# Moving the factor gb and a row term off VectorE in the last phase of an adaLN forward-and-backward kernel

## The chip, the cores and the metric

The kernel runs on one core of a Trainium2 chip. The time is device microseconds of that core, as the median of the runs; the profile is one execution, whose span runs from its first to its last instruction. The engines are called as the profile calls them: PE (TensorE matmuls), PEld (its weight loads), DVE (VectorE), ACT (ScalarE), POOL (GpSimd) and SP (SyncE, which here only issues transfers).

## The reference, cut to what matters

One block is computed with its whole backward pass: a spectral filter and a two-layer MLP (squared relu), each behind a LayerNorm that is modulated by vectors from `silu(c) @ w_mod`.

```python
sa, ca, ga, sb, cb, gb = chunks(silu(c) @ w_mod)      # six rows of 512
h = layernorm(x) * (1 + ca) + sa
x = x + ga * spectral(h, w_r, w_i)                    # x: 2048 x 512
h = layernorm(x) * (1 + cb) + sb
r = relu(h @ w1 + b1)                                 # 2048 x 1792
x = x + gb * ((r * r) @ w2 + b2)
# outputs: x, and the gradients of A_x, w_r, w_i, w1, b1, w2, b2, c, w_mod for a given grad_out
```

Two gradients matter here. With g = grad_out (2048 x 512) and H = r*r:

- grad w2 = H^T (g * gb) and grad b2 = the column sums of g * gb. Since gb belongs to the column, it can be applied to g before the product, or to the product after it.
- grad A_x, the last phase, is the backward pass of the first LayerNorm. For each row, with n the normalized row, s its incoming gradient times (1 + ca) and times 1/std: grad = s - mean(s) - n * mean(s * n), plus the gradient that comes past the block. `n * factor + offset`, with a factor and an offset for each row, is the term of the change's name.

## The kernel before

The kernel keeps rows as 128 partitions x 16 tiles x 512. A scheduler orders each engine's instructions by priority and estimated readiness, so that the order on an engine is near that of the program but not the same; `issue_after(X)` keeps an instruction from being placed ahead of X. Tiles come from pools with a number of buffers (`bufs`). A pool that opens where another was released waits for the last user of that memory.

The stage before the last is the backward of the spectral filter (`spec_f23`, eight steps gi). PE fills its gaps with units of grad w1 (`fill_w1`, L1126), and the gradient of w_mod is made by `gm.emit`, for four of six column blocks here:

```python
def ew_b(gi, G):
    ...                                              # DVE complex products; gW is stored by SP
def after_b(gi):
    if gi + 4 < 8:
        load(gi + 4)
    if gi == 3:
        with tc.issue_after(K["gW"]):
            nc.sync.dma_start(K["LG"], LG_dram)
    fill_w1(2 if 0 < gi < 6 else 1)
    if gi == 4:
        with tc.issue_after(K["gW"]):
            load_hn()                                # a transposed load of H, 128 x 2048
            load_hn()
    if gi == 5:
        gmp.release()
        endp["g"] = tc.alloc_tile_pool(name="gsp", bufs=1, side="right")
        endp["g_sb"] = endp["g"].tile([P, NT, D], BF16, name="g_sb")
        with tc.issue_after(K["gW"]):
            K["g_load"] = nc.sync.dma_start(endp["g_sb"], g_view).ins
    if gi in (0, 1, 3, 4):
        gms.pop(0)[1]()                              # gm.emit of one block
        if len(gms) > 1:
            gm.load(gms[1][0], gmp)
```

Then come the units of grad w2, here with the factor gb on the product, and the loads of the last phase's rows:

```python
def grad_w2(fc):
    ps = mmps.tile([P, SB], FP32, name="mm")
    for t in range(NT):                              # L1203
        nc.tensor.matmul(ps, lhsT=hns[fc][:, t, :], rhs=g_sb[:, t, :], start=(t == 0), stop=(t == NT - 1))
    gw = gwp.tile([P, D], BF16, name="gw", bufs=3)
    with tc.high_priority():                         # L1206
        nc.vector.tensor_tensor(gw, ps, modb[:, GB_B, :], op=ALU.mult)
    nc.sync.dma_start(out6_view[:, fc, :], gw)
    load_hn()
...
with tc.issue_after(K["g_load"]):
    load_rows3(0)                                    # n1 and gxl, two row tiles each
    load_rows3(2)
for _ in range(2):
    load_hn()
CS = utcs.tile([P, NT, 4, 16, 8], BF16, name="utcs")
spec_g1(tc, K, Z, CS)                                # PE L346; casts of the result: DVE L351, ACT L353
```

The last phase is a loop over eight pairs of row tiles. `fill(n)` gives PE n units in between: three of grad w1 that are left, then the 14 of grad w2.

```python
def row_pair(t, Ts):
    n1, gxl = rows3[t]
    ...
    for i in range(2):
        psY = spec_g3(tc, K, Ts[i], psE)             # PE L385; Ts was cast by ACT, L377
        nc.scalar.copy(out=gs[:, i, :], in_=psY)     # ACT L1276
    unfold(nc, fp, gh1, gs, 2, "unf_u")              # DVE L266 to L270
    nc.vector.tensor_tensor(gn, gh1, modb[:, CA1_B, ...], op=ALU.mult)                   # L1278
    for i in range(2):                               # ACT L1280, with the row's sum
        nc.scalar.activation(gs[:, i, :], gn[:, i, :], AF.Copy, scale=inv1[...], accum_out=rr[:, i, 0:1])
    nc.vector.tensor_tensor(q1, gh1, n1, op=ALU.mult)                                    # L1281
    late.add(lambda: colsums1(t, gh1, q1))           # PE L1262
    for i in range(2):                               # L1285, the row's sum of s * n
        nc.vector.scalar_tensor_tensor(out=jk, in0=gs[:, i, :], ..., in1=n1[:, i, :], ..., accum_out=rr[:, i, 1:2])
    nc.vector.tensor_scalar(rr[:, :, 2:4], rr[:, :, 0:2], -1.0 / D, None, op0=ALU.mult)
    for i in range(2):                               # L1289
        nc.vector.tensor_scalar(gn[:, i, :], n1[:, i, :], rr[:, i, 3:4], rr[:, i, 2:3], op0=ALU.mult, op1=ALU.add)
    nc.vector.tensor_tensor(gs, gn, gs, op=ALU.add)                                      # L1290
    nc.vector.tensor_tensor(gx, gs, gxl, op=ALU.add)                                     # L1292
    nc.sync.dma_start(out1_view[:, t:t + 2, :], gx)
    load_rows3(t + 4)

Ts = g2_pair(0)                                      # PE L375, ACT L377
for t in range(0, NT, 2):
    fill(1)
    row_pair(t, Ts)
    Ts = g2_pair(t + 2)
    fill(1 if t % 4 == 0 and t < 12 else 0)
    if t == 10:
        grad_b2()
fill(1)
late.flush()
...                                                  # column sums acc1 -> acc1_sb
fill(1)
for j in range(2):                                   # the last two blocks of grad w_mod
    gm.load(j, endp["gm"])
    gm.emit(j, 32 * j, acc1_sb[32 * j:32 * j + 1, :], endp["gm"], psX)
    fill(1)
while units2:
    fill(1)
...                                                  # grad c
```

Of the kernel before, what the change touches and what calls it, by code (L numbers as in the profile page):

```python
# [9 lines left out]
AF = mybir.ActivationFunctionType  # L10
ALU = mybir.AluOpType
# [7 lines left out]
D = 512  # L19
# [313 lines left out]
        f3(7)  # L333


def spec_g1(tc, K, Z, CS):
    nc = tc.nc
    with tc.tile_pool(name="psG", bufs=4, space=PSUM) as psG_pool, tc.tile_pool(name="psF", bufs=1, space=PSUM) as psF_pool:
        psF = psF_pool.tile([P, 4, P], FP32, name="psF")
        for gi in range(8):  # L340
            for hh in range(2):
                n = 2 * gi + hh
                ps = psG_pool.tile([P, 2, 2 * P], FP32, name="psG")
                for ch in range(2):
                    for ri in range(2):
                        nc.tensor.matmul(ps[:, ch, :], lhsT=Z[gi][:, hh, ri, ch:256:2],  # L346
                                         rhs=K["LG"][:, n, ri:ri + 2, :].rearrange("p y m -> p (y m)"), start=(ri == 0), stop=(ri == 1))
                dst = CS[:, :, :, n, :].rearrange("p t c b -> p c t b")
                src = ps.rearrange("p h (y t b) -> p (h y) t b", y=2, b=8)
                if hh == 0:  # L350
                    nc.vector.tensor_copy(out=dst, in_=src)  # L351
                else:
                    nc.scalar.copy(out=dst, in_=src)  # L353

            if gi % 2 == 1:
                for ri in range(2):
                    for n in range(2 * gi - 2, 2 * gi + 2):
                        q = 32 * (n % 4)
                        nc.tensor.matmul(psF[q:q + 1, n // 4, :], lhsT=Z[n // 2][:, n % 2, ri, 256:257], rhs=K["LG"][:, n, ri + 1, :],
                                         start=(ri == 0), stop=(ri == 1), tile_position=(0, q))  # L360
        for i in range(4):
            dst = CS[0:1, :, 1, i:16:4, :].rearrange("p t m b -> p m t b")
            src = psF[32 * i:32 * i + 1, :, :].rearrange("p m (t b) -> p m t b", b=8)
            if i % 2 == 0:
                nc.vector.tensor_copy(out=dst, in_=src)
            else:
                nc.scalar.copy(out=dst, in_=src)
# [76 lines left out]
class GMod:  # L444
# [10 lines left out]
        for dc in range(0, 4, 2):  # L455
            self.tc.nc.sync.dma_start(self.tiles[jc][dc // 2], self.wm_view[:, dc:dc + 2, cs])

    def emit(self, jc, q, row, pool, ppool):

        nc, K = self.tc.nc, self.K  # L460
        cs = slice(jc * D, (jc + 1) * D)
        psb = ppool.tile([P, D], FP32, name="mm")
        nc.tensor.matmul(psb, lhsT=K["ones_sq"][q:q + 1, :], rhs=row, start=True, stop=True, tile_position=(q, 0))
        gmbc = pool.tile([P, D], BF16, name="gmbc", bufs=1)
        nc.scalar.copy(out=gmbc, in_=psb)  # L465
        junk = pool.tile([P, D], BF16, name="gm_junk", bufs=1)
        for dc in range(0, 4, 2):
            wmc = self.tiles[jc][dc // 2]
            gwm = pool.tile([P, 2, D], BF16, name="gwm", bufs=2)
            for i in range(2):  # L470
                if i == 0:
                    nc.scalar.activation(gwm[:, i, :], gmbc, AF.Copy, scale=self.scf[:, dc + i:dc + i + 1])
                else:
                    nc.vector.tensor_scalar(gwm[:, i, :], gmbc, self.scf[:, dc + i:dc + i + 1], None, op0=ALU.mult)
                nc.vector.scalar_tensor_tensor(out=junk, in0=wmc[:, i, :], scalar=K["onef"], in1=gmbc, op0=ALU.mult, op1=ALU.mult,  # L475
                                               accum_out=self.gsc[:, jc, dc + i:dc + i + 1])
            nc.gpsimd.dma_start(self.out9_view[:, dc:dc + 2, cs], gwm)  # L477
# [3 lines left out]
def kernel(  # L481
# [585 lines left out]
            nc.sync.dma_start(hns[fc], h_dram[fc, :, :], transpose=True)  # L1067

    lf2 = tc.alloc_tile_pool(name="lf2", bufs=1, side="right")
    gmp = tc.alloc_tile_pool(name="gmp", bufs=1, side="right")  # L1070
    K["LF"] += [lf2.tile([P, 2, 3, P], BF16, name=f"LFb{gi}") for gi in range(4, 8)]
    W4 = 448
# [17 lines left out]
        nc.scalar.copy(out=b4, in_=ps[:, 0:W4])  # L1090
        nc.gpsimd.dma_start(out_5.rearrange("(q f) -> q f", q=NFB), b4[0:P:32, :])

    def add_quadrants(ps, pool, out, scale=None):
        w = ps.shape[-1]
        b4 = pool.tile([P, w], BF16, name="b4", bufs=1)
        b4l = pool.tile([P, w], BF16, name="b4l", bufs=1)
        nc.scalar.copy(out=b4, in_=ps)
        nc.vector.tensor_tensor(b4l, ps, b4, op=ALU.subtract)

        def add():  # L1100
            ps = mmps.tile([P, SB], FP32, name="mm")
            for i, x in enumerate((b4, b4l)):
                nc.tensor.matmul(ps[0:1, 0:w], lhsT=K["ones_col"], rhs=x, start=(i == 0), stop=(i == 1))
            row = pool.tile([1, w], BF16, name="b4r", bufs=2)
            nc.scalar.copy(out=row, in_=ps[0:1, 0:w])
            if scale is not None:
                nc.vector.tensor_tensor(row, row, scale, op=ALU.mult)
            nc.sync.dma_start(out, row)

        later.append([4, add])  # L1110
# [3 lines left out]
    def run_later(n=1):  # L1114
        if later:
            later[0][0] -= n
            if later[0][0] <= 0:
                later.pop(0)[1]()

    w1o = {}  # L1120

# [27 lines left out]
    with tc.tile_pool(name="f23b", bufs=2) as fr, tc.tile_pool(name="ewb", bufs=2) as ew:  # L1149
# [22 lines left out]
# [3 lines that stand above are left out]
            if gi == 3:  # L1175
                with tc.issue_after(K["gW"]):
                    nc.sync.dma_start(K["LG"], LG_dram)
            fill_w1(2 if 0 < gi < 6 else 1)
            if gi == 4:
                with tc.issue_after(K["gW"]):  # L1180
                    load_hn()
                    load_hn()
            if gi == 5:
                gmp.release()
                endp["g"] = tc.alloc_tile_pool(name="gsp", bufs=1, side="right")
                endp["g_sb"] = endp["g"].tile([P, NT, D], BF16, name="g_sb")
                with tc.issue_after(K["gW"]):
                    K["g_load"] = nc.sync.dma_start(endp["g_sb"], g_view).ins
            if gi in (0, 1, 3, 4):
                gms.pop(0)[1]()  # L1190
                if len(gms) > 1:
                    gm.load(gms[1][0], gmp)

        spec_f23(tc, K, UT, AEs, None, lambda gi: gwa.tile([P, 2, 2, FP], BF16, name="G", bufs=2), ew_b, after_b)
    g_sb = endp["g_sb"]
    fin = tc.alloc_tile_pool(name="fin", bufs=2, side="right")
    gwp = tc.alloc_tile_pool(name="gwp", bufs=1, side="right")
    endp["gw"] = gwp

# [3 lines that stand above are left out]
            nc.tensor.matmul(ps, lhsT=hns[fc][:, t, :], rhs=g_sb[:, t, :], start=(t == 0), stop=(t == NT - 1))  # L1203
        gw = gwp.tile([P, D], BF16, name="gw", bufs=3)
        with tc.high_priority():
            nc.vector.tensor_tensor(gw, ps, modb[:, GB_B, :], op=ALU.mult)  # L1206
        nc.sync.dma_start(out6_view[:, fc, :], gw)
        load_hn()

    def grad_b2():  # L1210
        ps = psX.tile([P, D], FP32, name="mm")
        for t in range(NT):
            q = 32 * (t % 4)
            nc.tensor.matmul(ps[q:q + 32, :], lhsT=K["ones_q"], rhs=g_sb[:, t, :], start=(t < 4), stop=(t >= 12), tile_position=(0, q))
        add_quadrants(ps, gwp, out_7[None, :], modb[0:1, GB_B, :])

    rows3 = {}

    def load_rows3(t):
        if t < NT:  # L1220
            rows3[t] = (fin.tile([P, 2, D], BF16, name="n1"), fin.tile([P, 2, D], BF16, name="gxl"))
            nc.sync.dma_start(rows3[t][0], n1_dram[:, t:t + 2, :])
            nc.sync.dma_start(rows3[t][1], gx1_dram[:, t:t + 2, :])

    with tc.issue_after(K["g_load"]):
        load_rows3(0)
        load_rows3(2)
    for _ in range(2):
        load_hn()

    CS = utcs.tile([P, NT, 4, 16, 8], BF16, name="utcs")
    spec_g1(tc, K, Z, CS)
    sp.release()
    lg2.release()
    fp = tc.alloc_tile_pool(name="fin2", bufs=2, side="right")
# [19 lines left out]
    with tc.tile_pool(name="psE", bufs=2, space=PSUM) as psE, tc.tile_pool(name="psS1", bufs=1, space=PSUM) as psS1:  # L1255
# [11 lines left out]
        def row_pair(t, Ts):  # L1267
# [18 lines left out]
                                               accum_out=rr[:, i, 1:2])  # L1286
            nc.vector.tensor_scalar(rr[:, :, 2:4], rr[:, :, 0:2], -1.0 / D, None, op0=ALU.mult)
            for i in range(2):
                nc.vector.tensor_scalar(gn[:, i, :], n1[:, i, :], rr[:, i, 3:4], rr[:, i, 2:3], op0=ALU.mult, op1=ALU.add)  # L1289
            nc.vector.tensor_tensor(gs, gn, gs, op=ALU.add)  # L1290
            gx = fp.tile([P, 2, D], BF16, name="gx")
            nc.vector.tensor_tensor(gx, gs, gxl, op=ALU.add)  # L1292
# [4 lines left out]
        for t in range(0, NT, 2):  # L1297
# [3 lines left out]
            fill(1 if t % 4 == 0 and t < 12 else 0)  # L1301
            if t == 10:
                grad_b2()
        fill(1)
        late.flush()
        acc1_odd = fp.tile([64, D], FP32, name="acc1_odd", bufs=1)
# [2 lines left out]
        nc.vector.tensor_tensor(acc1_sb, acc1[0:64, :], acc1_odd, op=ALU.add)  # L1309
        fill(1)  # L1310
        for j in range(2):
            gm.load(j, endp["gm"])
            gm.emit(j, 32 * j, acc1_sb[32 * j:32 * j + 1, :], endp["gm"], psX)
            fill(1)
        while units2:
            fill(1)
# [10 lines left out]
    psX.release()  # L1327
    fp.release()
    gwp.release()
    fin.release()  # L1330
    endp["g"].release()
    lf2.release()
    hnp.release()
    h2p.release()
# [37 lines left out]
```

## Time and profile before

| | value |
|---|---|
| time, median of 3 | 429.94 us (428.81 to 430.19) |
| span of the profiled run | 428.8 us |
| busy PE, DVE, ACT | 396.5, 354.7, 256.5 us |
| bytes moved by transfers | 101.11 MB |
| span from L1126's last units to the end | 345.39 to 428.8 us |

The page gives busy shares over the whole span, and they hide that the stages differ. PE is busy 92% overall, DVE 83%; which of them sets the pace is to be read stage by stage. In a line of groups the columns are the line of the program, the engine, the operation, output and inputs by name, the shapes and the count; then the busy time in us and the mean of one in ns; then the idle time of the engine just ahead of them, with what ended it. In a timeline the first column is the start and the second the length, both in us, and idle time ahead of the piece stands in brackets. An engine works through its queue in order, so a piece that waits holds up all behind it.

### The profile page before, as it was taken

To read this page: it belongs to the slowest core of one execution; us is meant where nothing else is said; L and a number is where in the kernel's file an instruction comes from. 1 tells how busy PE (TensorE), PEld (TensorE's weight loads), DVE (VectorE), ACT (ScalarE), POOL (GpSimd) and SP (SyncE) were. 2 spreads that over 40 slices of the span, in tenths; PEclk is the share of its full clock that TensorE was granted. 3 is DMA by queue.
4 is the path that set the end of the run, shared out by engine and by line. 5 is a ranking of instruction groups with operands and counts; after the bars stand their busy time and mean duration, and the time that the engine had idled before them with its cause. 6 is when DMAs were issued, how large, how long until landed. Compare 5 with 4: busy or idle time off the path is not lost.

```text
span 428.8 us, 7116 instructions
## 1 busy us (share of the span) xinstructions
PE 396.5 (92%) x2353; PEld 195.9 (46%) x2375; DVE 354.7 (83%) x862; ACT 256.5 (60%) x487; POOL 54.7 (13%) x135
## 2 busy tenths in 40 slices
PE   2789999999899999999999999999999999998894
PEld 0345446654434444444444444455555654443341
DVE  6799858959995588978897998947997946999994
ACT  5568699778882188248734856463756464536331
POOL 7347940000000000000000000002221000000011
PEclk9999999999999999999999999999999999999998
DMA  9997899969496469768965998979999999999993
GB/s 238 249 271 246 225 240 329 308 221 234 130 355 226 142 93 333 200 156 202 301 171 170 177 312 279 298 181 323 278 285 275 180 244 200 215 272 284 209 259 122
DMA packets 144227, 101.11 MB, mean 236 GB/s; under 512 B 98969, under 2 KB 127518, under 8 KB 143806
## 3 DMA queue, kind: packets, MB, share of 16 engines
q1 hardware_dynamic: 141034, 93.03, 82.6%
q0 software_dynamic: 2592, 7.09, 5.7%
q10 hardware_dynamic: 564, 0.53, 0.4%
q8 instruction: 19, 0.31, 0.3%
q14 instruction: 18, 0.15, 0.1%
HBM read 35.44 MB, written 41.60 MB: 180 GB/s over the span
## 4 chain that ended last, share of the span: by engine, by line
PE 47%; DVE 22%; ACT 15%; DMA 8%; issue 5%; POOL 1%; SPq 0%; ACTq 0%; DVEq 0%
PE og L906 12%; PE mm L877 10%; PE mm L1126 8%; PE mm L712 6%; DMA out_dram<-gW 2%; DMA n<-n_dram 2%; ACT gab L717 2%; PE psG L346 2%; DVE jk L1285 2%; PE psC L311 2%; ACT AE L329 1%; ACT Xs L313 1%; DMA out_dram<-gwm 1%; ACT AE L330 1%; DVE l_st L817 1%
## 5 line engine op out<-in xcount | busy, mean ns | idle before, releaser
L712 PE MATMUL mm<-gT,w2T 128*128 128x512 bf16 x224 | 57.9, 384 | 2.9 <-ACT gab L717 2.9
L877 PE MATMUL mm<-h2T,w 128*128 128x512 bf16 x224 | 53.4, 379 | 1.6 <-ACT r L879 1.4
L1203 PE MATMUL mm<-g_sb,hn 128*128 128x512 bf16 x217 | 50.1, 379 | 1.7 <-DVE gw L1206 1.2
L906 PE MATMUL og<-w1T,gab 128*128 128x512 bf16 x218 | 49.9, 379 | 1.0 <-DVE o L971 0.8
L1126 PE MATMUL mm<-gab,h_sb 128*128 128x448 bf16 x256 | 50.7, 352 | 0.0
L906 PE MATMUL og<-w,h 128*128 128x512 bf16 x217 | 49.1, 379 | 0.3
L879 ACT ACTIVATE r<-mm,b1col 128x512 bf16<-128x512 f32 x56 | 37.1, 686 | 6.1 <-PE mm L877 3.3
L877 PEld LDWEIGHTS <-w 128*128 128x128 bf16 x224 | 21.1, 97 | 30.0 <-issue 8.3
L1126 PEld LDWEIGHTS <-h_sb 128*128 128x128 bf16 x256 | 24.6, 98 | 21.8 <-issue 0.6
L1203 PEld LDWEIGHTS <-hn 128*128 128x128 bf16 x224 | 21.2, 98 | 28.3 <-issue 5.0
L906 PEld LDWEIGHTS <-h 128*128 128x128 bf16 x224 | 21.7, 98 | 26.1 <-issue 1.0
L906 PEld LDWEIGHTS <-gab 128*128 128x128 bf16 x224 | 21.6, 98 | 25.9 <-issue 1.4
L712 PEld LDWEIGHTS <-w2T 128*128 128x128 bf16 x224 | 21.3, 99 | 22.5 <-issue 6.5
L919 ACT CAST G<-og 128x512 bf16<-128x512 f32 x16 | 9.2, 581 | 28.0 <-PE og L906 28.0
L1280 ACT ACTIVATE gs<-gn,inv 128x512 bf16<-128x512 bf16 x16 | 11.4, 715 | 23.5 <-DVE gn L1278 23.5
L295 POOL MEMSET AE<- 128x2 bf16 x4 | 0.3, 102 | 193.7 <-DMA gx_dram<-n2rows 193.7
L477 POOL DMA_DIRECT2D out_dram<-gwm x12 | 8.8, 730 | 118.3 <-DVE gx L1292 56.9
L881 DVE TENSOR_TENSOR h<-r 128x1024 bf16<-128x1024 bf16 x28 | 19.3, 688 | 4.8 <-ACT r L879 4.8
L717 ACT CAST gab<-mm 128x512 bf16<-128x512 f32 x36 | 21.3, 600 | 2.0 <-PE mm L712 1.8
L475 DVE SCALAR_TENSOR_TENSOR gm_junk<-wmc,onef,gmbc 128x512 bf16<-128x512 bf16 x24 | 18.0, 748 | 3.5 <-ACT gmbc L465 1.9
L715 DVE CAST gab<-mm 128x512 bf16<-128x512 f32 x20 | 13.7, 687 | 8.0 <-PE mm L712 7.8
L377 ACT ACTIVATE Tsb<-psT 128x512 bf16<-128x512 f32 x32 | 18.5, 608 | 1.5 <-PE psT L375 1.0
(290 smaller groups left out, 802.3 us busy)
## 6 DMA issues: line engine op xcount, KB each, us to landing
h_dram<-h SPq DMA_DIRECT2D x28, 256.0 KB, 3.2
gh_dram<-gab SPq DMA_DIRECT2D x28, 256.0 KB, 4.3
w<-in_B_w_dram SPq DMA_DIRECT2D x2, 1792.0 KB
wmc<-in_w_mod_dram SPq DMA_DIRECT2D x12, 256.0 KB, 5.5
out_dram<-gwm POOLq DMA_DIRECT2D x12, 256.0 KB, 6.3
wz_dram<-Z SPq DMA_DIRECT2D x8, 258.0 KB, 4.4
xs_dram<-Xs SPq DMA_DIRECT2D x8, 258.0 KB, 4.2
Z<-wz_dram SPq DMA_DIRECT2D x8, 258.0 KB, 5.7
```

Source lines behind the costliest of these rows:

```text
L377: nc.scalar.activation(Tsb, ps, AF.Copy, scale=EF_S)
L475: nc.vector.scalar_tensor_tensor(out=junk, in0=wmc[:, i, :], scalar=K["onef"], in1=gmbc, op0=ALU.mult, op1=ALU.mult, accum_out=self.gsc[:, ...
L712: nc.tensor.matmul(ps, lhsT=w2T[:, dc, fc * P:(fc + 1) * P], rhs=gT[b][:, :, dc, :], start=(dc == 0), stop=(dc == 3))
L715: nc.vector.tensor_copy(out=gaT[b][:, fc, :], in_=ps)
L717: nc.scalar.copy(out=gaT[b][:, fc, :], in_=ps)
L877: nc.tensor.matmul(ps, lhsT=w1[:, dc, (fc + i) * P:(fc + i + 1) * P], rhs=h2T[b][:, :, dc, :], start=(dc == 0), stop=(dc == 3))
L879: nc.scalar.activation(r[:, i, :], ps, AF.Relu, bias=b1col[:, fc + i:fc + i + 1])
L881: nc.vector.tensor_tensor(h2, r, r, op=ALU.mult)
L906: nc.tensor.matmul(ps, lhsT=lhs(fc), rhs=rhs[:, fc, :], start=(fc == 0), stop=(fc == NFC - 1))
L1126: nc.tensor.matmul(ps[:, 0:W4], lhsT=h2_sb[:, t, dc * P:(dc + 1) * P], rhs=ghn[t // 4][:, t % 4, fs], start=(t == 0), stop=(t == NT - 1))
L1203: nc.tensor.matmul(ps, lhsT=hns[fc][:, t, :], rhs=g_sb[:, t, :], start=(t == 0), stop=(t == NT - 1))
L1280: nc.scalar.activation(gs[:, i, :], gn[:, i, :], AF.Copy, scale=inv1[:, t + i:t + i + 1], accum_out=rr[:, i, 0:1])
```

## The change

It has four parts.

1. **gb goes to the gradient.** g_sb is multiplied by gb in place, a quarter of the row tiles at a time, on DVE inside `spec_g1` (steps 4 to 7, behind the cast of that step). The evictions of grad w2 become plain copies on ACT, and grad b2 loses its factor.
2. **The row term goes to ACT**: an activation with scale and bias by row in place of DVE's tensor_scalar.
3. **Loads are placed earlier**: the rows of the first two pairs behind LG at step 3; the gradient at step 4 in four pieces, with the hn loads behind it; the last two w_mod blocks inside the loop. For that, the gm buffers are released at step 4, and the pool `fin` of the rows opens ahead of them.
4. **Four gwm buffers** in place of two for the last two blocks.

It is meant to relieve DVE in the last phase and to have the data there when it is needed. The loads and the matrix products are the same as before.

```diff
-def spec_g1(tc, K, Z, CS):
+def spec_g1(tc, K, Z, CS, after=None):
...
-                    nc.vector.tensor_copy(out=dst, in_=src)
+                    K["cast"] = nc.vector.tensor_copy(out=dst, in_=src).ins
...
+            if after:
+                after(gi)
...
-    def emit(self, jc, q, row, pool, ppool):
+    def emit(self, jc, q, row, pool, ppool, nbuf=2):
...
-            gwm = pool.tile([P, 2, D], BF16, name="gwm", bufs=2)
+            gwm = pool.tile([P, 2, D], BF16, name="gwm", bufs=nbuf)
...
+    fin = tc.alloc_tile_pool(name="fin", bufs=2, side="right")
     gmp = tc.alloc_tile_pool(name="gmp", bufs=1, side="right")
...
             if gi == 3:
                 with tc.issue_after(K["gW"]):
                     nc.sync.dma_start(K["LG"], LG_dram)
+                    load_rows3(0)
+                    load_rows3(2)
             fill_w1(2 if 0 < gi < 6 else 1)
+            if gi in (0, 1, 3, 4):
+                gms.pop(0)[1]()
+                if len(gms) > 1:
+                    gm.load(gms[1][0], gmp)
             if gi == 4:
-                with tc.issue_after(K["gW"]):
-                    load_hn()
-                    load_hn()
-            if gi == 5:
                 gmp.release()
                 endp["g"] = tc.alloc_tile_pool(name="gsp", bufs=1, side="right")
                 endp["g_sb"] = endp["g"].tile([P, NT, D], BF16, name="g_sb")
                 with tc.issue_after(K["gW"]):
-                    K["g_load"] = nc.sync.dma_start(endp["g_sb"], g_view).ins
-            if gi in (0, 1, 3, 4):
-                gms.pop(0)[1]()
-                if len(gms) > 1:
-                    gm.load(gms[1][0], gmp)
+                    for t in range(0, NT, 4):
+                        K["g_load"] = nc.sync.dma_start(endp["g_sb"][:, t:t + 4, :], g_view[:, t:t + 4, :]).ins
+                with tc.issue_after(K["g_load"]):
+                    load_hn()
+                    load_hn()
...
-            nc.vector.tensor_tensor(gw, ps, modb[:, GB_B, :], op=ALU.mult)
+            nc.scalar.copy(out=gw, in_=ps)
...
-        add_quadrants(ps, gwp, out_7[None, :], modb[0:1, GB_B, :])
+        add_quadrants(ps, gwp, out_7[None, :])
...
-    with tc.issue_after(K["g_load"]):
-        load_rows3(0)
-        load_rows3(2)
...
-    spec_g1(tc, K, Z, CS)
+
+    def scale_g(gi):
+        if gi >= 4:
+            gs = g_sb[:, 4 * gi - 16:4 * gi - 12, :]
+            with tc.issue_after(K["cast"]):
+                nc.vector.tensor_tensor(gs, gs, modb[:, GB_B, None, :].broadcast_to([P, 4, D]), op=ALU.mult)
+
+    spec_g1(tc, K, Z, CS, scale_g)
...
-                nc.vector.tensor_scalar(gn[:, i, :], n1[:, i, :], rr[:, i, 3:4], rr[:, i, 2:3], op0=ALU.mult, op1=ALU.add)
+                nc.scalar.activation(gn[:, i, :], n1[:, i, :], AF.Identity, scale=rr[:, i, 3:4], bias=rr[:, i, 2:3])
...
             if t == 10:
                 grad_b2()
+                gm.load(0, endp["gm"])
+                gm.load(1, endp["gm"])
...
-            gm.load(j, endp["gm"])
-            gm.emit(j, 32 * j, acc1_sb[32 * j:32 * j + 1, :], endp["gm"], psX)
+            gm.emit(j, 32 * j, acc1_sb[32 * j:32 * j + 1, :], endp["gm"], psX, 4)
```

More of the change, by code (lines that the diff above doesn't have):

```diff
@@ L1091, in grad_b1, with add_quadrants @@
         nc.gpsimd.dma_start(out_5.rearrange("(q f) -> q f", q=NFB), b4[0:P:32, :])
-    def add_quadrants(ps, pool, out, scale=None):
+    def add_quadrants(ps, pool, out):
         w = ps.shape[-1]
@@ L1105, in add @@
             nc.scalar.copy(out=row, in_=ps[0:1, 0:w])
-            if scale is not None:
-                nc.vector.tensor_tensor(row, row, scale, op=ALU.mult)
             nc.sync.dma_start(out, row)
@@ L1118, in run_later, with load_rows3 @@
                 later.pop(0)[1]()
+    rows3 = {}
+    def load_rows3(t):
+        if t < NT:
+            rows3[t] = (fin.tile([P, 2, D], BF16, name="n1"), fin.tile([P, 2, D], BF16, name="gxl"))
+            nc.sync.dma_start(rows3[t][0], n1_dram[:, t:t + 2, :])
+            nc.sync.dma_start(rows3[t][1], gx1_dram[:, t:t + 2, :])
     w1o = {}
@@ L1187, in after_b @@
                 with tc.issue_after(K["gW"]):
-                    K["g_load"] = nc.sync.dma_start(endp["g_sb"], g_view).ins
-            if gi in (0, 1, 3, 4):
-                gms.pop(0)[1]()
-                if len(gms) > 1:
-                    gm.load(gms[1][0], gmp)
+                    for t in range(0, NT, 4):
[3 more added lines that the diff above has]
+                    load_hn()
         spec_f23(tc, K, UT, AEs, None, lambda gi: gwa.tile([P, 2, 2, FP], BF16, name="G", bufs=2), ew_b, after_b)
     g_sb = endp["g_sb"]
-    fin = tc.alloc_tile_pool(name="fin", bufs=2, side="right")
     gwp = tc.alloc_tile_pool(name="gwp", bufs=1, side="right")
@@ L1214, in grad_b2 @@
             nc.tensor.matmul(ps[q:q + 32, :], lhsT=K["ones_q"], rhs=g_sb[:, t, :], start=(t < 4), stop=(t >= 12), tile_position=(0, q))
-        add_quadrants(ps, gwp, out_7[None, :], modb[0:1, GB_B, :])
[L1217 to L1223, printed above, removed]
-    with tc.issue_after(K["g_load"]):
-        load_rows3(0)
-        load_rows3(2)
+        add_quadrants(ps, gwp, out_7[None, :])
     for _ in range(2):
@@ L1329 @@
     gwp.release()
+    endp["g"].release()
     fin.release()
-    endp["g"].release()
     lf2.release()
```

## The prediction

> **What bounds the kernel now.** I read the page's first part, then its 40 slices to find where TensorE (PE) stops being full, then the busy time by stretch, the groups of the last 100 us, the waits of the same stretch and the timelines of each engine. All parts of the change lie behind 320 us.
>
> Busy time by stretch; columns are the stretch, its length, then busy us and instruction count of PE, PEld, DVE, ACT, POOL, then clock, DMA share and GB/s:
>
> ```profile
> 320.00:330.00 10.00, 10.00 (x71) 6.06 (x70) 7.51 (x19) 6.36 (x12) 2.00 (x3) 1.00 1.02 318
> ...
> 350.00:360.00 10.00, 9.95 (x61) 5.34 (x61) 5.44 (x14) 6.63 (x15) 1.08 (x2) 1.00 0.89 179
> ...
> 390.00:400.00 10.00, 8.20 (x45) 3.53 (x43) 9.87 (x23) 3.68 (x9) 0.00 (x0) 1.00 0.99 237
> 400.00:410.00 10.00, 7.53 (x37) 2.74 (x35) 9.51 (x23) 4.94 (x12) 0.00 (x0) 1.00 1.01 222
> ```
>
> Up to about 350 us PE has no holes. In the last phase VectorE (DVE) is full instead (9.87 of 10 us) while PE falls to 8.20 and 7.53, and ScalarE (ACT) is half idle. So the last phase is set by DVE, not by PE. The groups between 330 and 429 us say what DVE does there:
>
> ```profile
> L1280 ACT ACTIVATE gs<-gn,inv 128x512 bf16<-128x512 bf16 x16 | 11.4, 715 | 23.5 <-DVE gn L1278 23.5
> L1206 DVE TENSOR_TENSOR gw<-mm,modb 128x512 bf16<-128x512 f32 x14 | 9.6, 685 | 0.0
> L1289 DVE TENSOR_SCALAR gn<-n,rr 128x512 bf16<-128x512 bf16 x16 | 5.9, 408 | 0.1
> L1281 DVE TENSOR_TENSOR q<-gh,n 128x1024 bf16<-128x1024 bf16 x8 | 5.5, 688 | 3.6 <-DMA n<-n_dram 3.5
> ```
>
> The second and third are what the change takes from DVE. The first shows ACT idle 23.5 us in all behind a DVE product. The last shows a second wait: 3.05 us of the 3.5, at 356.56, is the first pair of normalized rows arriving late.
>
> PE's timeline shows where the end lies:
>
> ```profile
> 345.39 2.82 PE L1126 MATMUL mm<-gab,h_sb 128*128 128x448 bf16 x14
> ...
> 395.54 0.86 PE L385 MATMUL psY<-Tsb,TAT 128*128 128x512 bf16 x2 [1.64 <-ACT Tsb L377]
> ...
> 404.36 0.38 PE L1262 MATMUL acc<-gh,ones_q 128*32 128x512 bf16 x1 [1.18 <-DVE gh L270]
> ...
> 412.40 10.53 PE L1203 MATMUL mm<-g_sb,hn 128*128 128x512 bf16 x47
> ```
>
> The last weight-gradient product ends at 412.40 + 10.53 = 422.93, and the span ends 5.9 later, at 428.8.
>
> **What the skill says, and whether this trace agrees.** "VectorE: DVE Perf Modes", The perf-mode tier table: a two-tensor operation from SBUF in bf16 runs at two elements a cycle, with a PSUM operand at one, and a one-source operation in SBUF at four. The trace agrees: 685 ns for 512 elements from PSUM (L1206), 688 ns for 1024 from SBUF (L1281), 408 for 512 one-source (L1289). So the factor gb is cheaper applied to the gradient in SBUF than to products in PSUM, and the normalized term is DVE's cheapest kind: it costs more on ACT. "ScalarE: Activation LUTs", What ACT_TABLE_LOAD costs: each per-partition pointer operand adds about 93 ns. The same kind of operation, with scale and bias by row, stands in an earlier phase (L940): 808 ns, two in 1.52 us; one-pointer L1280 takes 715. That agrees. "Perfetto Trace Analysis", Optimizing Scalar/DVE Operations: DVE is faster where it has a mode, but with DVE saturated moving work to ScalarE may make sense. That is the case here; whether it pays no run has shown yet.
>
> **The change, part by part.** Neighbours overlap, so I count start-to-start distances, not durations.
>
> *DVE in the row loop.* From the first q (356.56) to the last (406.17) are seven pairs of rows in 49.6 us, 7.09 a pair. In that stretch lie nine gw of 0.60 (5.4 us) and 14 gn of 0.33 (4.6 us). Without them 39.6 remain, 5.66 a pair.
>
> *ACT in the row loop.* Now a pair costs 1.42 (two L1280 with their accumulator reads), 0.95 (two casts gs) and 0.95 (two Tsb): 3.3 us. Added: two gn at 0.72 = 1.44, and 9/7 evictions of gw at 0.49 (the spacing of the same kind of cast) = 0.63. That makes 5.4 a pair. ACT goes from half idle to nearly as loaded as DVE.
>
> *PE.* No matmul goes or comes. From 345.39 the work, if packed without holes, is: three remaining units of L1126 at 3.03 = 9.1; 14 products of 16 matmuls at (10.53 - 0.38)/47 = 0.216, 48.4; psT 8 x 0.46 = 3.7; psY 16 x 0.216 = 3.5; column sums 8 x 0.33 = 2.6; the rest 1.8. Sum 69.1, so PE cannot end before 414.5. It ended at 422.93: 8.4 us of holes is **all that this phase can give**, whatever DVE saves. The row loop holds three L1126 units, eight products and the small ones, 47.6 us over eight pairs: 5.95 a pair. So after the change PE, DVE and ACT stand at 5.95, 5.66 and 5.4 a pair: no engine has much slack, and each pair still crosses between DVE and ACT six times. Between the transforms and the products I allow PE about 2.5 us of the old holes to survive.
>
> *Added on DVE before the loop.* Four in-place products of 4 x 512 elements: 688 ns per 1024 at 0.60 spacing makes some 1.2 each, 4.9 in all. They stand between the casts of the second transform (L351, 338.9 to 345.5), where DVE has about 1.4 us of gaps, and it idles 3.66 us before 351.23 and again before 356.56. The casts of the last three groups come up to 3 us later; PE has L1126 units to do, but its queue is in order. I charge 1 us on PE.
>
> *The loads.* The first rows (four loads of 256 KB) go ahead, so the 3.05 us wait at 356.56 goes. The gradient's 2 MB load goes ahead of the hn transposes, and has to be there some 15 us earlier, since the scaling now stands before the loop. Bytes are the same, and the DMA engines are already full (share 1.02 from 320 to 330), so what is early pushes something late.
>
> *The end.* The w_mod loads go ahead, and four gwm buffers in place of two remove the wait for the store. ACT waited 2.7 us (L472), and the last store holds the end by 0.8. I count 0.8, so the tail is 5.1.
>
> *Sum.* PE's end 414.5 + 2.5 + 1 = 418.0; tail 5.1; span 423.1. The median time lies 429.94 - 428.8 = 1.1 above the span: 424.2, rounded to **424.0**.
>
> **The rivals.**
>
> *Late loads take the place of the late rows.* The queue of SyncE before:
>
> ```profile
> 326.11 11.38 SPq L1067 DMA_TRANSPOSE hn<-h_dram  x2
> ...
> 340.34 0.40 SPq L1188 DMA_DIRECT2D g_sb<-in_grad_out_dram  x1
> 340.83 9.60 SPq L1170 DMA_DIRECT2D out_dram<-gW  x8
> 350.93 0.33 SPq L1222 DMA_DIRECT2D n<-n_dram  x1
> ```
>
> g_sb lies where the gm buffers lay, so its load waits for their last store, issued at 325.94; a gwm store takes 6.3 us to land (the page), so about 332. Two MB at some 250 GB/s make 8 us: 340, just in time for the first scaling. If it comes at 346 to 350, DVE stands in front of it with casts behind, and PE with it. The gW stores and transposes follow later than now, and ACT's first Tsb already waits on a gW store (0.5 us). This rival gives back 3 to 7 us: 427 to 431. For it speaks the full DMA; against it, that the load was split in four and needs only a quarter at a time.
>
> *ACT becomes the bound.* If the crossings cost more than I allow, a pair takes 6.5 to 7 us and ACT's gw copies, put ahead by priority, hold up the row chain. The loop would gain only 1 to 4 us: 426 to 429. For it speaks the 5.4 beside 5.95; against it, that two pairs can be in work at once.
>
> *Everything packs.* PE without holes: 414.5 + 5.1 + 1.1 = 420.7. This is the floor, and only it and its neighbourhood lie under 421.3, 2% below the time before.
>
> **Range and chances.** Range 420.5 (the floor) to 429.5 (ACT or the loads eat nearly all). Faster by over 2% needs almost the whole of the 8.4 us of holes: 0.22. Slower by over 2% (438.5) needs a DVE stall of over 8 us with none of the gain: 0.03. The rest, 0.75, within 2%.
>
> **What would show it right or wrong.** Right: no DVE wait of 3 us on n; q every 6.0 to 6.3 us; ACT at 85 to 95% in the loop; DVE below 90%; PE above 95%; the last product ends at 417 to 419. Wrong in the load step: a DVE wait on the load of g_sb, or the casts L351 ending after 350. Wrong in the ACT step: PE waits on Tsb, or on gw from ACT, of several us in sum. Wrong in the floor: a last product that ends before 414.5, which would mean that PE's earlier stretch moved as well.

## The result and the profile after

The changed kernel took 433.04 us (median, 432.45 to 433.84) beside 429.54 for the kernel before (with a fourth run; 428.81 to 430.19). The ratio is 1.0083, with a 95% interval of 1.0058 to 1.0109: **slower by 0.8%**, where 424.0 in a range of 420.5 to 429.5 was predicted. The profiled spans are 431.5 and 428.8 us.

Busy time by stretch, with the columns of the first block of the prediction:

```profile
350.00:360.00 10.00, 9.81 (x66) 5.37 (x65) 4.72 (x11) 7.56 (x17) 1.04 (x2) 1.00 0.42 112
360.00:370.00 10.00, 9.28 (x51) 4.20 (x51) 9.43 (x23) 9.10 (x18) 0.00 (x0) 1.00 0.89 172
370.00:380.00 10.00, 5.19 (x32) 2.33 (x31) 3.38 (x10) 3.36 (x9) 0.00 (x0) 0.92 1.00 215
380.00:390.00 10.00, 8.84 (x40) 3.96 (x41) 8.49 (x19) 8.83 (x19) 0.00 (x0) 0.74 1.01 350
390.00:400.00 10.00, 9.95 (x74) 4.51 (x73) 7.13 (x17) 6.13 (x12) 0.00 (x0) 1.00 1.00 229
400.00:410.00 10.00, 8.05 (x42) 3.13 (x41) 9.34 (x23) 9.19 (x20) 0.00 (x0) 1.00 0.95 230
```

ACT is no longer half idle: 9.10 of 10 us from 360 and 9.19 from 400. But from 370 to 380 PE, DVE and ACT are all idle for about half of the time or more, and from 380 to 390 TensorE's granted clock is 0.74. No engine's load explains three idle engines; something from outside is missing. The groups between 330 and 432 us name it:

```profile
L1295 ACT ACTIVATE gn<-n,rr 128x512 bf16<-128x512 bf16 x16 | 12.3, 808 | 10.0 <-DVE rr L1293 6.6 <-issue 2.2 <-ACT gs L1282 0.8
L1286 ACT ACTIVATE gs<-gn,inv 128x512 bf16<-128x512 bf16 x16 | 11.5, 717 | 3.4 <-DVE gn L1284 3.4
L1296 DVE TENSOR_TENSOR gs<-gn,gs 128x1024 bf16<-128x1024 bf16 x8 | 5.5, 688 | 4.6 <-ACT gn L1295 4.5
L1287 DVE TENSOR_TENSOR q<-gh,n 128x1024 bf16<-128x1024 bf16 x8 | 5.5, 687 | 7.7 <-DMA n<-n_dram 7.7
```

The row term takes 808 ns on ACT (L1295), as expected. ACT's idle time ahead of `gs` fell from 23.5 to 3.4 us. New is the third line, where DVE waits 4.5 us for ACT's row term. The fourth is the surprise: DVE waits 7.7 us on the rows, where it was 3.5 before, though the change was to load them earlier. DVE's timeline shows when:

```profile
343.02 1.21 DVE L1236 TENSOR_TENSOR g_sb<-g_sb,modb 128x2048 bf16<-128x2048 bf16 x1
...
355.07 0.42 DVE L266 TENSOR_TENSOR unf_u<-gs 128x512 bf16<-128x512 bf16 x1 [3.66 <-ACT gs L1282]
...
376.38 0.69 DVE L1287 TENSOR_TENSOR q<-gh,n 128x1024 bf16<-128x1024 bf16 x1 [6.58 <-DMA n<-n_dram]
```

The first is one of four scalings of g_sb, 1.21 us each, 4.8 in all. The loop's first piece begins at 355.07; before, it was 351.23. So the first pair no longer waits for its rows (first q at 357.26, before 356.56), but what it gained there went to the scaling. The third line is the third pair: it waits 6.58 us. The queue of SP says why:

```profile
334.20 2.98 SPq L1200 DMA_DIRECT2D g_sb<-in_grad_out_dram  x4
337.23 9.36 SPq L1069 DMA_TRANSPOSE hn<-h_dram  x2
346.70 8.66 SPq L1179 DMA_DIRECT2D out_dram<-gW  x12
359.52 13.57 SPq L1069 DMA_TRANSPOSE hn<-h_dram  x5
373.19 0.52 SPq L1126 DMA_DIRECT2D n<-n_dram  x1
```

The second column is the time that issuing took. Five transposed loads stand in a row and hold the queue for 13.57 us, and behind them stands the load of the third pair's rows, issued at 373.19. Before, two transposed loads stood ahead of it and it went out at 363.25:

```profile
356.25 6.90 SPq L1067 DMA_TRANSPOSE hn<-h_dram  x2
363.25 0.53 SPq L1222 DMA_DIRECT2D n<-n_dram  x1
```

In the changed kernel the rows come, the chain starts again, and PE gets its next input:

```profile
380.94 1.07 PE L387 MATMUL psY<-Tsb,TAT 128*128 128x512 bf16 x2 [5.74 <-ACT Tsb L379]
...
383.74 7.59 PE L1213 MATMUL mm<-g_sb,hn 128*128 128x512 bf16 x31 [0.22 <-issue]
...
417.57 10.53 PE L1213 MATMUL mm<-g_sb,hn 128*128 128x512 bf16 x47
```

PE stood still for 5.74 us, named as a wait for ACT's Tsb, whose own delay began at the rows. The last product ends at 417.57 + 10.53 = 428.10 (before 422.93). Two-microsecond stretches show a second price (columns as above, the clock ahead of the last two):

```profile
376.00:378.00 2.00, 0.00 (x0) 0.00 (x0) 1.52 (x4) 0.00 (x0) 0.00 (x0) 1.00 0.79 96
378.00:380.00 2.00, 0.00 (x0) 0.00 (x0) 1.86 (x7) 1.11 (x2) 0.00 (x0) 0.60 1.21 332
380.00:382.00 2.00, 1.06 (x6) 0.17 (x5) 1.89 (x4) 1.54 (x4) 0.00 (x0) 0.50 0.98 294
...
384.00:386.00 2.00, 2.00 (x8) 0.76 (x7) 1.86 (x7) 1.84 (x4) 0.00 (x0) 0.69 1.05 341
386.00:388.00 2.00, 2.00 (x11) 0.94 (x10) 1.86 (x5) 1.74 (x4) 0.00 (x0) 1.00 0.98 354
```

While PE waits its clock falls to a half, and it gets going again at that clock. The page "TensorE: Matmul & The Clock Gate" of the Trainium skill, Part 1: The HAM clock gate, says that the clock is halved after an idle window of about 3.4 us and restored after as much busy time. The trace agrees with the half (0.50), and with the delay roughly: PE stopped at 375.20, and the mean of 0.60 from 378 to 380 puts the drop near 378.4, 3.2 us later.

**The account.** The first unit of grad w1 starts 0.51 us later than before (280.85, 280.34), so of the 5.17 us by which the last product is late, 4.7 belong to the last phase. By the stretches PE idles 8.9 us from 350 to its last product and idled 5.3 before: 3.6 us more. The other 1.1, by difference, I put down to pieces that ran at the lower clock; one of them is the 7.59 us above, for products that take 7.07 at full clock. The tail from the last product to the end shrank from 5.9 to 3.4 us. Sum: +0.5 + 4.7 - 2.5 = +2.7, the difference of the spans.

### The profile page after: what moved, and what is told of

The parts are those of the page before. It is cut to its first block, busy times and chain, and to the rows that moved or that the text cites. A ratio compares the mean times of both kernels' runs of the same rounds, so it can differ in the third digit from the quotient of the medians.

```text
span 431.5 us, 7133 instructions
## 1 busy us (share of the span) xinstructions
PE 397.7 (92%) x2353; PEld 196.4 (46%) x2375; DVE 346.2 (80%) x835; ACT 275.1 (64%) x517; POOL 54.8 (13%) x135
## 5 line engine op out<-in xcount | busy, mean ns | idle before, releaser
L1139 ACT CAST gw<-mm 128x448 bf16<-128x448 f32 x16 | 8.7, 541 | 20.4 <-PE mm L1135 20.4
```

## The experiments

Theory (Q in the expectations): the place of the rows in SP's queue, behind transposed loads, costs the time. First rival (A): the row term on ACT costs it, through ACT's load and the crossing; A2 is Q and A together. Second rival (D): what is loaded early takes bandwidth from what comes later. Third rival: there was little to win, whatever the queue does. S, from e9 on, is the theory that part 1 brings the bad order of the queue.

All ratios are against the kernel before on the same chip, whose median was 428.77 to 429.24 us. "Ahead" is the number of transposed loads between the loop's start and the third pair's rows. The column us is the median of all runs, while the ratio leaves out the runs in a slower state of the chip and is not the quotient of the medians, which for e4 would be 1.0025.

| run | kernel | us | ratio [95%] | ahead |
|---|---|---|---|---|
| e1 | changed, rows ahead of the transposes | 430.01 | 1.0031 [1.0007, 1.0055] | 2 |
| e2 | e1, row term on DVE | 427.83 | 0.9973 [0.9950, 0.9995] | 2 |
| e3 | changed, row term on DVE | 431.96 | 1.0065 [1.0041, 1.0090] | 5 |
| e4 | before, row term on ACT | 429.98 | 0.9995 [0.9970, 1.0021] | 3 |
| e5 | changed, rows loaded by POOL | 432.76 | 1.0075 [1.0048, 1.0103] | other queue |
| e6 | e5, row term on DVE | 432.98 | 1.0069 [1.0040, 1.0099] | other queue |
| e7 | e6, scaling behind all casts | 431.53 | 1.0059 [1.0034, 1.0084] | other queue |
| e8 | before, rows loaded by POOL | 430.93 | 1.0033 [1.0013, 1.0052] | other queue |
| e9 | parts 3 and 4 alone | 427.88 | 0.9969 [0.9949, 0.9989] | 2 |
| e10 | e9, row term on ACT | 430.92 | 1.0036 [1.0004, 1.0067] | 3 |
| e11 | e2, scaling behind all casts | 427.93 | 0.9963 [0.9943, 0.9983] | 2 |
| e12 | third row buffer, scaling late, row term on DVE | 428.27 | 0.9978 [0.9955, 1.0001] | 0 |

A single profile strays by some microseconds from the median of its kernel, so the ratios judge and the profiles explain.

### e1 and e2: the queue's order alone, then the row term too

```diff
-            nc.sync.dma_start(rows3[t][0], n1_dram[:, t:t + 2, :])
+            K["n1", t] = nc.sync.dma_start(rows3[t][0], n1_dram[:, t:t + 2, :]).ins
...
-            nc.sync.dma_start(hns[fc], h_dram[fc, :, :], transpose=True)
+            with tc.issue_after(K["n1", 4] if fc in (4, 5, 6) else K["gW"]):
+                nc.sync.dma_start(hns[fc], h_dram[fc, :, :], transpose=True)
...
-                gm.load(0, endp["gm"])
-                gm.load(1, endp["gm"])
+                with tc.issue_after(K["n1", 6]):
+                    gm.load(0, endp["gm"])
+                    gm.load(1, endp["gm"])
```

> The changed kernel with only the order of SP's queue altered: the fifth to seventh transposed load of H (hn) stands behind the load of the third pair's normalized rows, and the two late w_mod loads behind the fourth pair's. Theory Q (queue order: that load stood behind five transposes, 13.6 us of issue time, and DVE, then PE, waited on it): the wait of 6.6 us on n goes, PE's 5.7 us hole and the slow clock behind it (some 1.9 us) with it; 425 to 426 us. Theory A (the row term on ACT lengthens each pair's chain): nothing changes, 431 to 434. Theory D (what is loaded early takes bandwidth from what comes later): a late load is only moved to another place, 430 to 433.

Measured 1.0031, some 0.5% less than the changed kernel. DVE's waits on rows shrank to 0.73 and 0.51 us, PE waits 1.5 us at most, and the clock is 1.00 throughout. So the order of the queue makes up more than half of the loss by these ratios, but not all; their intervals allow from a fifth to the whole. The time lies in D's range, above Q's 425 to 426, but no other load came late in place of the rows. In e1's timeline of DVE a different wait remains:

```profile
388.61 0.69 DVE L1297 TENSOR_TENSOR gs<-gn,gs 128x1024 bf16<-128x1024 bf16 x1 [2.12 <-ACT gn L1296]
...
411.08 0.69 DVE L1297 TENSOR_TENSOR gs<-gn,gs 128x1024 bf16<-128x1024 bf16 x1 [2.35 <-ACT gn L1296]
```

Where DVE has nothing else to do, it stands over 2 us until ACT has made the row term; on DVE the two pieces took 0.73 (0.33 + 0.41). e2 is e1 with the row term back:

```diff
-                nc.scalar.activation(gn[:, i, :], n1[:, i, :], AF.Identity, scale=rr[:, i, 3:4], bias=rr[:, i, 2:3])
+                nc.vector.tensor_scalar(gn[:, i, :], n1[:, i, :], rr[:, i, 3:4], rr[:, i, 2:3], op0=ALU.mult, op1=ALU.add)
```

> As e1_order, with the row term back on DVE (part 2 of the change undone). Theory Q: near e1_order, 424 to 428, since what DVE takes back (0.65 us a pair) it has free. Theory A: clearly faster than e1_order, by 4 us or more. Theory D: as e1_order, 430 to 433.

Measured 0.9973, 0.6% less than e1, some 2.5 us. So with the rows in time, the row term on ACT **costs** 2.5 us. Both Q and A hold a share, and D, which expected 430 to 433 here too, does not fit.

### e3 and e4: the row term alone, from either side

e3 is the changed kernel with the edit just shown; e4 is the kernel before with the reverse of it.

> The changed kernel with only the row term back on DVE; the five transposes still stand ahead of the third pair's rows. Theory Q: as the changed kernel, 431 to 434, with a wait on n of 5 to 7 us on DVE. Theory A: 425 to 428. Theory D: 431 to 434 as well.

> The kernel before with only the row term on ACT (part 2 alone). Three transposes stand ahead of the third pair's rows here, in the kernel before two. Theory Q: 427 to 431, the relief of DVE (some 4.6 us of work in the loop) against one more transpose. Theory A: slower than before, 433 or more. Theory D: 426 to 428, as nothing was moved among the early loads.

e3 measured 1.0065, no clear gain over the changed kernel. With five transposes ahead DVE's wait is still there, as e3's timeline shows:

```profile
376.22 0.69 DVE L1287 TENSOR_TENSOR q<-gh,n 128x1024 bf16<-128x1024 bf16 x1 [6.06 <-DMA n<-n_dram]
```

So ACT's share is not the wait at the third pair; under a jammed queue the engine of the row term hardly counts. e4 measured 0.9995, no difference: what DVE saves (4.6 us of row terms by the prediction's count) and what the crossings cost seem to cancel there, where the rows come in time (DVE waits 0.64 us on n). e4's profile holds a piece of evidence on the clock, in two-microsecond stretches:

```profile
398.00:400.00 2.00, 0.00 (x0) 0.00 (x0) 1.97 (x7) 1.13 (x3) 0.00 (x0) 1.00 0.96 239
400.00:402.00 2.00, 1.71 (x4) 0.43 (x4) 2.00 (x5) 0.72 (x2) 0.00 (x0) 0.59 1.16 268
402.00:404.00 2.00, 2.00 (x7) 0.77 (x6) 1.92 (x5) 1.52 (x4) 0.00 (x0) 0.55 1.01 295
```

PE had stood still for 2.48 us ending at 400.29, and the clock fell to 0.59 and 0.55 just when it was back at work.

### e9 and e10: the loads and buffers alone

Against the changed kernel:

```diff
-            nc.scalar.copy(out=gw, in_=ps)
+            nc.vector.tensor_tensor(gw, ps, modb[:, GB_B, :], op=ALU.mult)
...
-    spec_g1(tc, K, Z, CS, scale_g)
+    spec_g1(tc, K, Z, CS)
```

and grad b2 with its factor again. e9 also has the row term on DVE; e10 has it on ACT.

> Parts 3 and 4 of the change alone (the earlier loads and the four gwm buffers); gb stays on the products and the row term on DVE, as before. The order of SP's queue then has two transposes ahead of the third pair's rows, as in the kernel before; so what put five there is part 1. Theory S (part 1 delays the first pair by 3.8 us on DVE, its row buffer comes free later, and the queue fills with transposes first): no wait of several us on n, the loop starts 3 us earlier than before; 425.5 to 428. Theory D (early loads harm by themselves): 430 to 434.

> As e9_loads_only, with the row term on ACT (the change without part 1). Three transposes stand ahead of the third pair's rows. Theory S: 425 to 428, within 1.5 us of e9_loads_only either way; the row term on ACT is no loss where DVE is full. If the row term on ACT itself is harmful: 2 us or more above e9_loads_only.

e9 measured 0.9969: parts 3 and 4, with nothing taken from DVE, are faster than the kernel before, so the early loads do no harm in sum (D). In its queue two transposed loads stand ahead of the rows instead of five:

```profile
355.46 4.69 SPq L1069 DMA_TRANSPOSE hn<-h_dram  x2
360.20 0.58 SPq L1128 DMA_DIRECT2D n<-n_dram  x1
```

DVE waits on no rows, and the last product ends at 419.12. e10 measured 1.0036, 0.7% or 2.9 us more than e9, as expected if the row term on ACT is itself harmful, with three transposes ahead, 5.8 us of waits on rows and 3.7 us of DVE's waits on ACT's row term. So with the row term on ACT one more transposed load stands ahead of the rows, as in e4 beside the kernel before. That ACT's later release of the row buffer is the reason is argued.

Part 1, the scaling with the evictions on ACT, is the difference between e9 and e3 (2 and 5 ahead) and between e10 and the changed kernel (3 and 5). With it the loop starts later, the buffers of the rows come free later, and the scheduler, which writes the order of the queue, puts the transposes ahead, which need only an hn buffer. That part 1 brings the five is shown; the way through the later start is argued, and the scaling was not tried apart from the evictions.

### e5 to e8: the rows through another queue

The edit of e5, against the changed kernel:

```diff
-            nc.sync.dma_start(rows3[t][0], n1_dram[:, t:t + 2, :])
+            eng = nc.sync if t < 4 else nc.gpsimd
+            eng.dma_start(rows3[t][0], n1_dram[:, t:t + 2, :])
...
-            nc.sync.dma_start(rows3[t][1], gx1_dram[:, t:t + 2, :])
+            eng.dma_start(rows3[t][1], gx1_dram[:, t:t + 2, :])
```

> The changed kernel with the row loads of the loop (third pair on) issued by POOL, whose queue holds nothing else there, so that no transpose stands ahead of them. Theory Q alone: waits on n vanish, and the row term on ACT costs nothing: 424 to 425.5, equal to e6_rows_pool_gnDVE. Theory A2 (queue order first, and behind it the row term on ACT, which costs more than it frees once the rows are there): still better than the changed kernel, but 2 us or more above e6_rows_pool_gnDVE: 426.5 to 428.5. Under both, no slow clock.

Measured 1.0075, as slow as the changed kernel and outside what either theory expected. The wait on n went away and came back as another; first DVE's line, then the queue of SP:

```profile
382.70 0.69 DVE L1299 TENSOR_TENSOR gx<-gs,gxl 128x1024 bf16<-128x1024 bf16 x1 [6.87 <-DMA out_dram<-gx]
```

```profile
358.70 14.62 SPq L1069 DMA_TRANSPOSE hn<-h_dram  x5
...
376.36 0.57 SPq L1300 DMA_DIRECT2D out_dram<-gx  x1
```

The first gx, ready at 365, is stored at 376.36, behind the same five transposes, so DVE had no gx buffer to write to. "The rows are late" was thus too narrow: whatever goes through the queue is late. The page "DMA: Bandwidth & Descriptors", Issuing engines are not separate DMA queues, says that issuing from several engines only saves the time of issuing, usually small relative to the transfer. Here that time is not small: in the changed kernel SP needs 143 us of the 431 for 62 transposed loads, 2.3 us each, and 0.5 for each of its other 247 transfers. The 14 loads of hn take 3.1 us each to issue, beside a median of 5.4 from issue to landing.

e6 has the row term on DVE besides (the edit of e2), e7 the four scalings behind all casts as well:

```diff
-    spec_g1(tc, K, Z, CS, scale_g)
+    spec_g1(tc, K, Z, CS)
+    for gi in range(4, 8):
+        scale_g(gi)
```

e8 is the kernel before with POOL's queue for the rows.

> As e5_rows_pool, with the row term back on DVE. Theory Q alone: as e5_rows_pool, 424 to 426. Theory A2: 424 to 426 here, and e5_rows_pool 2 us or more above it. If SP's queue was no cause at all, 430 or more.

> As e6_rows_pool_gnDVE, with the four scalings of the gradient behind all casts of the second transform, where DVE waits 3.7 us for the first rows. If the 3.8 us later start of the row loop counts (DVE sets the loop), 2 to 3 us faster than e6: 421.5 to 423.5. If PE sets it, less than 1 us: 424 to 425.5.

> The kernel before with the row loads of the loop on POOL. DVE waits there only 0.5 us on rows inside the loop (the 3.05 us wait is on the first pair, which SP still loads), so under both theories 428.5 to 430, the same as before. If POOL's queue itself were the gain (one more queue for everything), 426 or less.

Measured 1.0069, 1.0059 and 1.0033: none is faster than before, and all three lie above what was expected. e6 was to take 430 us or more if SP's queue were no cause, and it took 432.98; but the stores of gx still stand behind the transposed loads there (3.46 us of a DVE wait on one), so it does not clear that queue. e8 adds nothing but the queue and is 0.3% slower; its n and gxl, issued by POOL, landed in 4.9 and 6.0 us by the median, those of the kernel before, issued by SP, in 4.1 and 3.7. Whether that is all of e8's loss is open. Moving the rows is no cure.

### e11 and e12: is it the start of the loop, or the rows, that still holds the gain back?

e11 is e2 with e7's edit: the loop's casts no longer wait for the scaling. e12 has e7's edit, the row term on DVE and a third row buffer in place of the forced order (for room, the unused product of L1291 is written into gn):

```diff
+            pool = fin if t % 6 < 4 else endp["finx"]
-            rows3[t] = (fin.tile([P, 2, D], BF16, name="n1"), fin.tile([P, 2, D], BF16, name="gxl"))
+            rows3[t] = (pool.tile([P, 2, D], BF16, name="n1"), pool.tile([P, 2, D], BF16, name="gxl"))
...
+    load_rows3(4)                                        # ahead of the loop
...
-            load_rows3(t + 4)
+            load_rows3(t + 6)
```

> e2_order_gnDVE with the four scalings of the gradient behind the casts of the second transform, so that the row loop starts about 2.5 us earlier. If the start of the loop counts: 425 to 426.5. If PE's work sets the time by now: as e2_order_gnDVE, 427 to 428.

> The changed kernel with the row term back on DVE, the four scalings behind all casts, and a third buffer for the rows, so that the third pair's rows are asked for before the loop starts and no row waits for a buffer to come free just ahead of a transposed load. Theory that late rows are what still keeps the better order from its gain: no DVE wait on n over 0.5 us, no PE hole over 2 us, clock 1.00 throughout, 425 to 427 us, 0.990 to 0.994 of the kernel before. Rival, that the loop is set by the crossings between DVE, ACT and PE and by DVE's own work whatever the rows do: the n waits go too, but 427.5 to 428.5, 0.996 to 0.999, with the lost time in waits of DVE and PE on each other's results.

e11 measured 0.9963, not to be told from e2, as expected if PE's work sets the time by now. Its first q comes at 353.98 instead of 358.14 (2.5 us earlier with the starts aligned), but two waits on rows (1.64 and 1.85 us) and a PE wait of 2.46 us with a slower clock behind it stand against that in its profile. e12 measured 0.9978: DVE waits on no rows, the third pair's rows go out at 356.49 ahead of all the loop's transposes, PE's longest wait is 1.73 us and the mean clock 0.999. All that the theory of late rows asked for is there, its 0.990 to 0.994 is not. That theory falls for this last part; the rival is within its numbers. e12's stretches say what is left:

```profile
380.00:390.00 10.00, 9.95 (x74) 4.50 (x73) 8.91 (x21) 5.00 (x11) 0.00 (x0) 1.00 0.98 299
390.00:400.00 10.00, 8.01 (x41) 3.16 (x40) 9.18 (x23) 7.37 (x17) 0.00 (x0) 1.00 0.99 264
400.00:410.00 10.00, 7.83 (x35) 2.77 (x35) 9.50 (x26) 5.25 (x11) 0.00 (x0) 1.00 0.96 237
```

PE is full up to 390 and then idles 1.99 + 2.17 = 4.2 us, with no late data. The kernel before idled 4.3 us in the same two stretches. The loop's last pairs have fewer fill units (`t % 4 == 0 and t < 12`), and PE waits there for ACT's Tsb (1.73 us) and DVE's gh (1.69). DVE is still busy for 9.18 and 9.50 of 10 us, so these runs do not tell whether the pair's chain of crossings or DVE's own work sets the pace.

## Why the prediction was wrong, point by point

**The step that failed is the loads.** It said: "Bytes are the same, and the DMA engines are already full (share 1.02 from 320 to 330), so what is early pushes something late." It then sought the late thing at g_sb only. The rival named after it, late loads, had the right kind and the wrong victim: the casts did not wait for g_sb. What came late was the third pair's rows, and not for want of bandwidth but for their place in the queue: in e5, on POOL's queue beside the same five transposed loads, they were issued at 363.15, and q ran at 370.44 without a wait. The kernel before showed the two things needed: two transposed loads took 11.38 us to issue, and rows were asked for only when a buffer came free. The prediction never counted what would stand ahead of the rows once the loop moved: five transposed loads of 13.57 us, for which DVE waited 6.58 us and PE 5.74.

**The row term on ACT was priced by its busy time alone.** "Two gn at 0.72 = 1.44" was right (1.52 for two, 808 ns each). Unpriced were the crossing, 2.1 us of DVE's time where nothing else is ready against 0.73, and the later release of the rows. e2 to e1 and e9 to e10 put it at 2.5 and 2.9 us of loss, the second with late rows in it; in the kernel before (e4) it cost nothing clear. "Each pair still crosses between DVE and ACT six times" gave the crossings no price, and by the code part 2 adds two of them to the chain: rr to ACT, gn back to DVE. The prediction also took the 408 ns of L1289 for agreement with four elements a cycle. In the same trace a two-tensor operation of that size takes as long:

```profile
L266 DVE TENSOR_TENSOR unf_u<-gs 128x512 bf16<-128x512 bf16 x8 | 3.4, 421 | 3.8 <-ACT gs L1276 3.7
```

So the row term ran no faster on DVE than an operation counted at two a cycle. The sums used its measured spacing of 0.33 and are not touched.

**The size of the prize was wrong too.** "It ended at 422.93: 8.4 us of holes" came from a sum of spacings, 69.1 us of packed work. By the stretches, PE idled only 0.05 + 0.42 + 0.37 + 0.05 + 1.80 + 2.47 + 0.16 = 5.3 us from 350 on, so packed work ends near 417.6, not 414.5. e9 gives the same: 419.12 less 2.3 us idle is 416.8, with a start 0.5 earlier. The pieces between products cost more than their spacing in a long run; which of them, I did not settle. With the tail of 3.4 and the 1.1 of the prediction, a version without any hole would by this estimate stand at 417.6 + 3.4 + 1.1 = 422.1.

**DVE's pace was right where data were there.** Predicted was q every 6.0 to 6.3 us. In the changed kernel the distances are 5.97, 13.15, 6.55, 5.85, 9.33, 5.96 and 5.68: four of seven below that, one of 6.55, one with the late rows in it, and one, 9.33, while PE is full for most of it. The freed DVE time brought no earlier end, because from 350 to 390 PE had only 0.9 us of holes to start with. The gain had to come from 390 to 410, and there less work on DVE brought none that shows: e2, with part 1, measured 0.9973, and e9, without it, 0.9969. That the chain of the pair sets the pace there is argued.

**The scaling.** 4 x 1.21 = 4.84 us as predicted (4.9); the loop started 3.84 us later, 3.3 with the starts aligned; charged for the casts was "up to 3". PE did not feel it: the first product comes 0.1 us later when the starts are aligned, where I charged 1.

**The n wait at 356.56 went away**, as said, and in e9, where only loads and buffers differ, the last product came 3.3 us earlier with the starts aligned, in one profile. The ratio shows 1.3 us.

**The tail** became 3.4 us; predicted 5.1. In e9, with DVE's evictions, it is 5.2, so loads and buffers gave 0.7 of the 0.8 expected, and the rest came with the copies on ACT, as far as single profiles tell.

**What stays open.** No version reached 424. The best, 0.9963 to 0.9978, cannot be told apart. A schedule with fill units kept for the last pairs was not tried, and neither was a pair with fewer crossings, so what holds the loop from 390 to 410 is open.

## What to carry to other kernels

Before moving work that shifts a loop's start, write down the order in which one queue will issue its transfers, with the time of each issue: a few slow issues ahead of a small load can cost more than the engine time saved. Price work on another engine by the chain, crossing and buffer release included, and not by its busy time. Read an engine's holes from the stretches in which they lie, and ask for each who could fill it; time saved on DVE from 350 to 390, beside a full PE, was worth nothing here.

## What the runs showed of the hardware

- In the changed kernel a transposed load of H (128 x 2048) held SP's queue for 3.1 us on average, between 2.0 and 6.6, five in a row for 13.57; a plain transfer for 0.5. All that stands behind waits, stores included. Whether the whole of that time is issuing, or part of it a wait for room further down, the trace does not tell.
- A hole in PE's work brought the half clock at less than the 3.4 us of the page named above: 2.48 us in e4 (stretches of 0.59 and 0.55), 2.46 in e11 (0.69 and 0.50). But the length of the hole alone does not decide. A hole of 2.49 us in e10 left the clock at 1.00; first its line, then the stretch:

```profile
406.12 0.38 PE L1270 MATMUL acc<-gh,ones_q 128*32 128x512 bf16 x1 [2.49 <-DVE gh L270]
```

```profile
400.00:410.00 10.00, 7.51 (x39) 2.89 (x37) 9.76 (x22) 6.20 (x14) 0.00 (x0) 1.00 0.95 240
```

- By half-microsecond stretches the half clock lasted 3.41 us in e4 and in e11, and 6.83, twice that, in the changed kernel. That looks like a decision taken once in every 3.4 us, so that the place of a hole in this rhythm counts too; the runs fit it, but none was made to test it.
